# Two token tiles to a numerator matmul, and the order of the loop around it: a hedgehog linear-attention block with a token mixer on one core

## The chip, the core and the metric

The kernel runs on one core of a Trainium2 chip. The metric is the device time of one execution in microseconds (us). Engines: TensorE (PE in the profile, its weight loads PEld), VectorE (DVE), ScalarE (ACT), GpSimd (POOL), and SyncE (SP), which issues most of the transfers. Each engine works through its own list of instructions in order.

## The reference

```
x:    (1, 2048, 512), 32 heads of width 16
q, k, v = layernorm(x) @ wqkv
phi(u)  = [softmax(u @ w_phi), softmax(-(u @ w_phi))]        per head, 32 features
kv, z   = phi(k)^T v, sum of phi(k) over the tokens
num     = phi(q) kv
den     = phi(q) z + 1e-6
h       = x + (num / den) @ wo
u       = gelu(layernorm(layernorm(h))^T @ w1 + b1)          w1: (2048, 1792), along the tokens
out     = h + (u @ w2 + b2)^T                                w2: (1792, 2048)
```

All in float32.

## The kernel before

A token tile is 128 tokens, so there are NT = 16. Most float32 products are made of three matmuls in a faster 32-bit format (`mm3`, L60): each operand is split into a rounded part (`hi`, written by ScalarE) and the remainder (`lo`, a subtraction), and hi·hi, hi·lo and lo·hi are summed.

The first stage (to about 143 us of the span) makes phi(k), kv and z over all tiles, and projects q for some tiles on the way. The last one (from 387 us) is the second mixer product. Between them lies the loop of L630, `for it in range(NT + 3)`, which the change rewrites. It takes every tile through a pipeline, with a different tile at each step of one iteration:

- `q_mm` projects q for a tile (12 matmuls of 512 columns into one of two PSUM buffers, `pu`). Ten of the 16 tiles are left to this stage, six of them to the loop.
- `q_logits` (through `logit_ops`, L137) reads that buffer four times: VectorE takes the maximum (`mx`) and the minimum (`mn`) of each head and writes `v - mx` (the shift); ScalarE copies `v` raw into the other half of the tile (L147), and `negate` on GpSimd turns the copy into `mn - v`. `q_exp` then runs exp over both on ScalarE, and `q_sums` sums them on VectorE.
- `s_ez` (GpSimd) and `s_den` (VectorE: `tz`, `den`, `w`) make the weight that normalizes phi(q) and divides by den at once, and `s_pq` (GpSimd) multiplies phi(q) by it.
- `s_tr` transposes the tile's phi(q) on TensorE (8 transposes into the PSUM tile `tn`, L525), and two ScalarE copies bring it to SBUF as `pht` (L527).
- `s_num` multiplies with kv: 16 matmuls of 64 rows by 32 columns of weights and 128 moving columns, eight of them side by side in the array (L543, again into `tn`). Its result is split into `oh` (ScalarE) and `ol` (VectorE, `s_ol`).
- `s_wo` is the output projection, 12 matmuls of 512 columns into the one buffer `po`. `s_h` adds x and stores h, `s_moments`, `s_rstd` and `s_hn` normalize it and split it into `hs`.
- `fill` is the first mixer product: 12 matmuls for a token tile and a pair `p` of 128-feature blocks. In the loop it fills TensorE's time for pairs 0 and 1, LAG iterations behind the tile; all the rest follows after the loop. `stream` loads two tiles' weights (SP), `whi` is a ScalarE copy (L604), and `flush` makes `wlo` on VectorE (L596). Four buffers each hold `wraw`, `whi` and `wlo`.

From L419 on, `tc.manual_schedule` is in force: TensorE, VectorE, ScalarE and GpSimd execute in the order in which the code records the operations, until the loop ends (`ms.close()`). A framework places the semaphore waits from what each operation reads and writes; where two engines read the same PSUM tile, the one recorded later waits for the one recorded earlier. `turns` interleaves lists of VectorE operations, and `run` records them.

In one iteration TensorE's order is: num(it - 1), wo(it - 2), tr(it), then q_mm or fills.

Of the kernel before, what the change touches and what calls it, by code (L numbers as in the profile page):

```python
# [9 lines left out]
F32 = mybir.dt.float32  # L10
F32R = mybir.dt.float32r
AF = mybir.ActivationFunctionType
# [5 lines left out]
P = 128  # L18
# [4 lines left out]
NG = 8  # L23
# [1 line left out]
Q_AT = (4, 6, 8, 9, 11, 13)  # L25
V_NOT = (0, 1, 11)
SUMS = 8
LAG = 4
WARM = 9
EPS = 1e-5  # L30

# [2 lines left out]
def block_kernel(ctx: ExitStack, tc: tile.TileContext, x, xT, wT, phic, wo, w1, b1, w2, b2,  # L34
# [25 lines left out]
    def mm3(o, ah, al, bh, bl, first, last):  # L60

        nc.tensor.matmul(o, ah, bh, start=first, stop=False)  # L62
        nc.tensor.matmul(o, ah, bl, start=False, stop=False)  # L63
        nc.tensor.matmul(o, al, bh, start=False, stop=last)  # L64
# [72 lines left out]
    def logit_ops(src, e, pool):  # L137

        v = src.rearrange("p (j h d) -> p j h d", h=2, d=DH)
        ev = signs(e)  # L140
        mx = wk.tile([P, NPR, 2], F32, name="mx")
        mn = wk.tile([P, NPR, 2], F32, name="mn")

        def shift():
            nc.vector.tensor_sub(ev[:, :, 0], v, mx.unsqueeze(3).to_broadcast([P, NPR, 2, DH]))
            if pool:
                nc.scalar.activation(ev[:, :, 1], v, AF.Copy)  # L147
                MN.append((ev, mn))
            else:
                nc.vector.tensor_sub(ev[:, :, 1], mn.unsqueeze(3).to_broadcast([P, NPR, 2, DH]), v)  # L150

        return [lambda: nc.vector.tensor_reduce(mx, v, axis=AX.X, op=ALU.max),
                lambda: nc.vector.tensor_reduce(mn, v, axis=AX.X, op=ALU.min),
                shift]
# [7 lines left out]
    def turns(*lists):  # L162

        return [ops[i] for i in range(max(map(len, lists))) for ops in lists if i < len(ops)]

    def run(*lists):
        for op in turns(*lists):
            op()
# [192 lines left out]
    def q_mm():  # L361
        if q["mm"] < NT:
            PS[q["mm"]] = proj(q["mm"], wqh, wql, ps_q, "pu")
            q["mm"] += 1

    def q_logits(lag):
        n = q["logits"]
        if n < min(NT, q["mm"] - lag + NT * (q["mm"] == NT)):
            EQ[n] = big.tile([P, NG, P], F32, name="eq", tag="big")
            q["logits"] += 1  # L370
            return logit_ops(PS[n], EQ[n], n >= len(Q_AT))
        return []
# [71 lines left out]
    def s_den(t):  # L444


        tz = az.tile([P, NPR, 2, 2], F32, name="tz")
        den = az.tile([P, NPR, 2], F32, name="den")
        W[t] = az.tile([P, NPR, 2, 2], F32, name="w", bufs=3)
        other = SQ[t]  # L450
        return [lambda: nc.vector.reduce_sum(tz.rearrange("p g c h -> p (g c h)"), heads(EZ[t]), axis=AX.X),
                lambda: nc.vector.scalar_tensor_tensor(tz[:, :, 0], other[:, :, 1], 1e-6, tz[:, :, 0],
                                                       op0=ALU.mult, op1=ALU.add),
                lambda: nc.vector.tensor_mul(tz, other, tz),
                lambda: nc.vector.reduce_sum(den, tz.rearrange("p g c h -> p g h c"), axis=AX.X),
                lambda: nc.vector.reciprocal(den, den),
                lambda: nc.vector.tensor_mul(W[t], other, den.unsqueeze(2).to_broadcast([P, NPR, 2, 2]))]  # L457

    def s_pq(t):
        nc.gpsimd.tensor_mul(heads(EQ[t]), heads(EQ[t]), W[t].rearrange("p g c h -> p (g c h)").unsqueeze(2).to_broadcast([P, 2 * H, DH]))  # L460

    def lead(it, mm):

        if 0 <= it + 3 < NT:
            s_ez(it + 3)
        negate()
        for _ in range(mm):
            q_mm()
        q_exp(0)
# [49 lines left out]
    HN, HT, PHT, OS, PO, VE = {}, {}, {}, {}, {}, {}  # L519

    def s_tr(t):
        PHT[t] = ak.tile([P, NG, P], F32, name="pht")
        ptr = ps_t.tile([P, 2, 4, P], F32, name="tn")
        for g in range(NG):
            nc.tensor.transpose(ptr[:, g // 4, g % 4, :], EQ[t][:, g, :], ident)  # L525
        for half in range(2):
            nc.scalar.activation(PHT[t][:, half * 4:half * 4 + 4, :], ptr[:, half], AF.Copy)  # L527

    def s_kv():

        pt = ps_o.tile([P, 2, P], F32, name="po")
        for b in range(2):
            nc.tensor.transpose(pt[:, b, :], kvS[:, 2 * b:2 * b + 2, :].rearrange("p n f -> p (n f)"), ident)
        nc.scalar.activation(kvB, pt, AF.Copy)

    def s_num(t):

        pn = ps_t.tile([P, 2, 4, P], F32, name="tn")[:, :, 0:2]
        for b in range(2):
            for c in range(4):  # L540
                for r in range(2):
                    rows, cols = slice(64 * r, 64 * r + 64), slice(32 * c, 32 * c + 32)
                    nc.tensor.matmul(pn[cols, r, b, :], kvB[rows, b, cols], PHT[t][rows, 4 * b + c, :],  # L543
                                     start=True, stop=True, skip_group_check=True)
        oh = ak.tile([P, 2, 2, P], F32R, name="oh")
        ol = ak.tile([P, 2, 2, P], F32R, name="ol")
        nc.scalar.activation(oh, pn, AF.Copy)
        OS[t] = oh, ol, pn

    def s_ol(t):  # L550
        oh, ol, pn = OS[t]
        return [lambda: nc.vector.tensor_sub(ol, pn, oh)]

    def s_wo(t):
        oh, ol, _ = OS.pop(t)
        PO[t] = po = ps_o.tile([P, D], F32, name="po")
        for j in range(4):
            mm3(po, oh[:, j // 2, j % 2, :], ol[:, j // 2, j % 2, :], woh[:, j, :], wol[:, j, :], j == 0, j == 3)

    def s_x(t):  # L560
        HT[t] = ak.tile([P, D], F32, name="h", bufs=4)
        nc.sync.dma_start(HT[t], x[t * P:(t + 1) * P, :])
# [8 lines left out]
    def s_moments(t):  # L571

        junk = ak.tile([P, D], F32, name="hj", bufs=1)
        nc.scalar.activation(VE[t][:, 1:2], VE[t][:, 2:3], AF.Copy, scale=-1.0 / D)
        nc.scalar.activation(junk, HT[t], AF.Square, bias=VE[t][:, 1:2], accum_out=VE[t][:, 3:4])
        nc.scalar.activation(VE[t][:, 0:1], VE[t][:, 3:4], AF.Identity, scale=(1.0 + EPS) / D, bias=eps2)

    def s_rstd(t):
        nc.gpsimd.tensor_tensor(r2[:, t:t + 1], VE[t][:, 0:1], mhalf[:, :1], op=ALU.pow)
        nc.gpsimd.tensor_mul(VE[t][:, 1:2], VE[t][:, 1:2], r2[:, t:t + 1])  # L580
# [12 lines left out]
    def flush():  # L593
        while LATER:
            wl_, raw, wh_ = LATER.pop(0)
            LO.append(nc.vector.tensor_sub(wl_, raw, wh_).ins)  # L596
# [14 lines left out]
    def fill_load(p):  # L611
        if FL[p] < NT:
            WI[p, FL[p]] = stream(w1v, FL[p], 2, p * 256, 256)
            FL[p] += 2

    def fill(p, pool=None):

        t = FN[p]
        FN[p] = t + 1
        if FL[p] <= t:  # L620
            fill_load(p)
            flush()
        if t == 0:
            PU[p] = [pool.tile([P, D], F32, name="pu", tag="pu") for _ in range(2)]
        a, b = WI[p, t - t % 2]
        for c in range(2):
            mm3(PU[p][c], a[:, t % 2, c * P:(c + 1) * P], b[:, t % 2, c * P:(c + 1) * P],
                HN[t][:, 0], HN[t][:, 1], t == 0, t == NT - 1)

    for it in range(NT + 3):  # L630
        if 0 <= it < NT:
            s_x(it)
        if 0 <= it - 1 < NT:
            s_num(it - 1)
        if 0 <= it - 3 < NT:
            s_moments(it - 3)
        if 0 <= it - 2 < NT:
            s_wo(it - 2)
        if it == 1:
            run(q_logits(0))  # L640
            q_mm()
        if 0 <= it < NT:
            s_tr(it)
        if it == 0:
            s_kv()
        if 0 <= it + 1 < NT:
            s_pq(it + 1)
        if 0 <= it - 3 < NT:
            s_rstd(it - 3)
        lead(it, 1)  # L650
        den = s_den(it + 2) if it + 2 < NT else []
        ops = turns((s_ol(it - 1) if 0 <= it - 1 < NT else []) + q_logits(1) + (q_sums(0) if it > 0 else []), den)

        ops[3:3] = ([lambda: s_h(it - 2)] if 0 <= it - 2 < NT else []) + [flush]
        run(ops)
        if it > 0:
            negate()
        if 0 <= it - 3 < NT:
            s_hn(it - 3)
        if FN[0] <= it - LAG:  # L660
            fill(0, ps_f)
        for _ in range(2):
            if q["logits"] == NT and FN[1] <= it - LAG:
                fill(1, ps_q)
        for p in range(2):
            if it >= LAG - 2 and FL[p] <= FN[p] + 1:
                fill_load(p)
    flush()
    ms.close()
# [197 lines left out]
```

## Time and profile before

| what | us |
| --- | --- |
| median of 3 runs (lowest, highest) | 535.25 (534.66, 535.86) |
| the profiled execution | 535.27, its span 533.5 |
| PE, PEld busy | 523.4, 451.0 |
| DVE, ACT, POOL busy | 382.5, 277.6, 228.3 |
| numerators, L543, in the loop | 256 matmuls in 512 records, 0.60 a tile |
| fills, L62 to L64 into `pu` | 672 matmuls, about 0.39 each, started 0.228 apart |
| granted TensorE clock | 0.999 |

The span runs from the first to the last instruction. A matmul's duration holds the time in which it is pipelined with its neighbours, so two starts tell more of the pace than two durations. Line numbers in profile lines are those of the kernel before; in the changed kernel the same statements stand a line or a few lines further down.

### The profile page before, as it was taken

How to read it: one execution, taken by the hardware profiler on the slowest of the kernel's cores; microseconds unless marked ns; L12 is line 12 of the kernel's file. 1: busy time of each engine (PE TensorE's matmuls, PEld its weight loads, DVE VectorE, ACT ScalarE, POOL GpSimd, SP SyncE). 2: the span in 40 equal slices, each digit the busy share in tenths (PEclk: the TensorE clock that was granted, in tenths of full speed). 3: DMA queues.
4: the chain of work that ended last, by engine and by line, in shares of the span. 5: the costliest groups of instructions: out<-in, count | busy, mean ns of one | idle time of the engine just before them, and what ended most of it. 6: DMA issues, size and time to landing. Idle time of an engine off the chain costs nothing.

```text
span 533.5 us, 9887 instructions
## 1 busy us (share of the span) xinstructions
PE 523.4 (98%) x3872; PEld 451.0 (85%) x3872; DVE 382.5 (72%) x680; ACT 277.6 (52%) x470; POOL 228.3 (43%) x180
## 2 busy tenths in 40 slices
PE   8999999999999899999999999999999999999995
PEld 7888888887877777778788888888899999999995
DVE  6893999878798979784235523835768878887784
ACT  6998833525447777666766423525443343343340
POOL 2589699877876978985345000000001101100110
PEclk9999999999999999999999999999999999999999
DMA  8544310022302223333355333533014556535631
GB/s 303 196 124 119 86 35 21 1 62 78 101 1 83 95 81 119 120 109 111 95 159 182 99 100 99 159 111 87 20 41 110 138 149 146 131 120 120 158 78 43
DMA packets 45487, 55.85 MB, mean 105 GB/s; under 512 B 3968, under 2 KB 33024, under 8 KB 45440
## 3 DMA queue, kind: packets, MB, share of 16 engines
q1 hardware_dynamic: 43136, 51.38, 30.3%
q0 software_dynamic: 2016, 3.67, 5.1%
q8 instruction: 30, 0.49, 0.4%
q10 hardware_dynamic: 288, 0.17, 0.1%
q14 instruction: 17, 0.14, 0.1%
HBM read 46.81 MB, written 8.39 MB: 103 GB/s over the span
## 4 chain that ended last, share of the span: by engine, by line
PE 90%; DVE 5%; ACT 3%; issue 1%; POOL 1%; DVEq 0%; ACTq 0%; POOLq 0%
PE py L761 26%; PE pu L62 12%; PE pu L64 12%; PE pu L63 11%; PE po L62 3%; PE pv L63 2%; PE tn L525 2%; PE pv L64 2%; PE pv L62 2%; PE pk_ps L62 2%; PE po L63 2%; PE po L64 2%; PE pk_ps L64 2%; PE pk_ps L63 2%; PE tn L543 2%; PE kvp L207 1%
## 5 line engine op out<-in xcount | busy, mean ns | idle before, releaser
L799 POOL DMA_DIRECT2D out<-ot x14 | 12.5, 1001 | 212.1 <-DVE ot L797 212.1
L761 PE MATMUL py<-uf,whi 128*128 128x256 f32 x560 | 96.2, 283 | 0.0
L62 PE MATMUL pu<-hs,whi 128*128 128x512 f32 x224 | 87.6, 394 | 0.7 <-ACT eq L147 0.7
L57 ACT ACTIVATE whi<-wraw 128x1792 fp32r<-128x1792 f32 x28 | 47.7, 1705 | 77.9 <-PE py L761 62.9
L63 PE MATMUL pu<-hs,whi 128*128 128x512 f32 x224 | 87.2, 389 | 0.0
L64 PE MATMUL pu<-hs,wlo 128*128 128x512 f32 x224 | 87.0, 390 | 0.2 <-DVE wlo L596 0.2
L761 PEld LDWEIGHTS py<-uf,whi 128*128 128x128 f32 x560 | 83.3, 192 | 0.0
L596 DVE TENSOR_TENSOR wlo<-wraw,whi 128x512 fp32r<-128x512 f32 x56 | 46.3, 841 | 45.2 <-ACT whi L604 44.0
L761 PE MATMUL py<-uf,wlo 128*128 128x256 f32 x280 | 69.9, 283 | 0.0
L58 DVE TENSOR_TENSOR wlo<-wraw,whi 128x1792 fp32r<-128x1792 f32 x28 | 56.6, 2023 | 17.8 <-ACT whi L57 17.8
L604 ACT ACTIVATE whi<-wraw 128x512 fp32r<-128x512 f32 x56 | 34.4, 627 | 45.6 <-PE pu L63 41.6
L62 PEld LDWEIGHTS pu<-hs,whi 128*128 128x128 f32 x224 | 42.1, 188 | 9.3 <-ACT eq L147 1.2
L64 PEld LDWEIGHTS pu<-hs,wlo 128*128 128x128 f32 x224 | 42.1, 188 | 9.3 <-DVE wlo L596 0.6
L761 PEld LDWEIGHTS py<-uf,wlo 128*128 128x128 f32 x280 | 49.7, 192 | 0.0
L63 PEld LDWEIGHTS pu<-hs,whi 128*128 128x128 f32 x224 | 42.1, 188 | 8.4
L442 POOL TENSOR_TENSOR ez<-eq,zB 128x1024 f32<-128x1024 f32 x16 | 39.5, 2474 | 0.1
L761 PE MATMUL py<-un,whi 128*128 128x256 f32 x224 | 38.4, 283 | 0.0
L195 POOL TENSOR_TENSOR pk<-pk,sk 128x1024 f32<-128x1024 f32 x16 | 31.1, 1944 | 9.8 <-DVE sk L194 9.0
L460 POOL TENSOR_TENSOR eq<-eq,w 128x1024 f32<-128x1024 f32 x16 | 31.0, 1940 | 5.9 <-DVE w L457 5.9
L527 ACT ACTIVATE pht<-tn 128x512 f32<-128x512 f32 x32 | 17.4, 596 | 30.8 <-PE tn L525 30.8
L761 PEld LDWEIGHTS py<-un,whi 128*128 128x128 f32 x224 | 33.2, 192 | 0.1
L199 POOL TENSOR_TENSOR zacc<-zacc,pk 128x1024 f32<-128x1024 f32 x13 | 31.3, 2406 | 0.6
(165 smaller groups left out, 1192.8 us busy)
## 6 DMA issues: line engine op xcount, KB each, us to landing
wraw<-in_w SPq DMA_DIRECT2D x112, 256.0 KB, 2.9
xraw<-in_xT SPq DMA_DIRECT2D x16, 256.0 KB, 3.1
xh<-in_x SPq DMA_DIRECT2D x16, 256.0 KB, 2.6
h<-in_x SPq DMA_DIRECT2D x16, 256.0 KB, 3.1
out<-h SPq DMA_DIRECT2D x16, 256.0 KB, 2.0
out<-ot POOLq DMA_DIRECT2D x14, 256.0 KB, 4.6
wraw<-in_wT SPq DMA_DIRECT2D x12, 256.0 KB, 5.0
wo<-in_wo SPq DMA_DIRECT2D x4, 256.0 KB, 4.7
```

What stands on the lines that cost most here:

```text
L57: nc.scalar.activation(hi, src, AF.Copy)
L58: lo_engine.tensor_sub(lo, src, hi)
L62: nc.tensor.matmul(o, ah, bh, start=first, stop=False)
L63: nc.tensor.matmul(o, ah, bl, start=False, stop=False)
L64: nc.tensor.matmul(o, al, bh, start=False, stop=last)
L195: nc.gpsimd.tensor_mul(heads(PK[t]), heads(PK[t]), sk.unsqueeze(2).to_broadcast([P, 2 * H, DH]))
L199: nc.gpsimd.tensor_add(zacc, zacc, PK[t])
L442: nc.gpsimd.tensor_mul(EZ[t], EQ[t], zB)
L460: nc.gpsimd.tensor_mul(heads(EQ[t]), heads(EQ[t]), W[t].rearrange("p g c h -> p (g c h)").unsqueeze(2).to_broadcast([P, 2 * H, DH]))
L596: LO.append(nc.vector.tensor_sub(wl_, raw, wh_).ins)
L604: nc.scalar.activation(wh_, raw, AF.Copy)
L761: nc.tensor.matmul(o, a[x], b[:, y], start=start and i == 0, stop=stop and i == 2, skip_group_check=True)
```

## The change

The numerator is made for two token tiles at once: `pht` holds the transposes of a pair, and each of the 16 matmuls moves 256 columns, in every second iteration. The result is evicted by tile (`oh[:, i]`, `ol[:, i]`). `pht`, `oh` and `ol` have one buffer each in place of two.

The loop body is written anew. TensorE's order in an even iteration is num of the last two tiles, q_mm or fills, wo(it - 2), tr(it); in an odd one q_mm or fills, tr(it), wo(it - 2). So a q tile or fills stand between num and wo. The GpSimd product `s_pq` comes first in an iteration. On VectorE the two `ol` halves with the first step of den between them come first after num, then logits, flush and sums interleaved with the rest of den, and `s_h` last. The normalization `s_hn` of two tiles goes to the even iteration, one behind num and one at the end. The raw copy of q is recorded ahead of VectorE's reductions. LAG is 5 in place of 4, weights of pair 1 are asked for two iterations later than those of pair 0 and both one step further ahead, and `fill` flushes whenever the part that it needs is still in LATER.

```diff
-LAG = 4
+LAG = 5
...
     def logit_ops(src, e, pool):
...
+        if pool:
+            nc.scalar.activation(ev[:, :, 1], v, AF.Copy)
 
         def shift():
             nc.vector.tensor_sub(ev[:, :, 0], v, mx.unsqueeze(3).to_broadcast([P, NPR, 2, DH]))
             if pool:
-                nc.scalar.activation(ev[:, :, 1], v, AF.Copy)
                 MN.append((ev, mn))
...
     def s_tr(t):
-        PHT[t] = ak.tile([P, NG, P], F32, name="pht")
+        j, i = divmod(t, 2)
+        if i == 0:
+            PHT[j] = ak.tile([P, NG, 2, P], F32, name="pht", bufs=1)
...
-            nc.scalar.activation(PHT[t][:, half * 4:half * 4 + 4, :], ptr[:, half], AF.Copy)
+            nc.scalar.activation(PHT[j][:, half * 4:half * 4 + 4, i, :], ptr[:, half], AF.Copy)
...
-    def s_num(t):
-        pn = ps_t.tile([P, 2, 4, P], F32, name="tn")[:, :, 0:2]
+    def s_num(j):
+        pn = ps_t.tile([P, 2, 4, P], F32, name="tn")
...
-                    nc.tensor.matmul(pn[cols, r, b, :], kvB[rows, b, cols], PHT[t][rows, 4 * b + c, :],
+                    nc.tensor.matmul(pn[cols, r, 2 * b:2 * b + 2, :], kvB[rows, b, cols], PHT[j][rows, 4 * b + c, :, :],
                                      start=True, stop=True, skip_group_check=True)
-        oh = ak.tile([P, 2, 2, P], F32R, name="oh")
-        ol = ak.tile([P, 2, 2, P], F32R, name="ol")
-        nc.scalar.activation(oh, pn, AF.Copy)
+        oh = ak.tile([P, 2, 2, 2, P], F32R, name="oh", bufs=1)
+        ol = ak.tile([P, 2, 2, 2, P], F32R, name="ol", bufs=1)
+        pv = pn.rearrange("p r (b i) s -> p i r b s", i=2)
+        for i in range(2):
+            nc.scalar.activation(oh[:, i], pv[:, i], AF.Copy)
...
-        return [lambda: nc.vector.tensor_sub(ol, pn, oh)]
+        return [lambda i=i: nc.vector.tensor_sub(ol[:, i], pv[:, i], oh[:, i]) for i in range(2)]
...
     def fill(p, pool=None):
...
         if FL[p] <= t:
             fill_load(p)
+        if any(part is WI[p, t - t % 2][1] for part, _, _ in LATER):
             flush()
...
+    def fills(it):
         if FN[0] <= it - LAG:
             fill(0, ps_f)
         for _ in range(2):
             if q["logits"] == NT and FN[1] <= it - LAG:
                 fill(1, ps_q)
+
+    for it in range(NT + 3):
+        even = it % 2 == 0
+        if 0 <= it + 1 < NT:
+            s_pq(it + 1)
+        if it == 0:
+            s_tr(0)
+            s_kv()
+        if it == 1:
+            run(q_logits(0))
+            q_mm()
+            s_tr(1)
+        if it > 1 and even:
+            if it <= NT:
+                s_num(it // 2 - 1)
+            if it >= 4:
+                s_hn(it - 4)
+        den = s_den(it + 2) if it + 2 < NT else []
+        if it > 1 and even and it <= NT:
+            ol = s_ol(it // 2 - 1)
+            run(ol[:1] + den[:1] + ol[1:])
+            den = den[1:]
+        if it < NT:
+            s_x(it)
+        if it + 3 < NT:
+            s_ez(it + 3)
+        negate()
+        q_mm()
+        fills(it)
+        q_exp(0)
+        logits = q_logits(1)
+        if it >= 3 and even:
+            s_moments(it - 3)
+        if it > 1 and even and it - 2 < NT:
+            s_wo(it - 2)
+        if 1 < it < NT:
+            s_tr(it)
+        if it > 1 and not even and it - 2 < NT:
+            s_wo(it - 2)
+        if it >= 3 and not even:
+            s_moments(it - 3)
+        if it >= 3:
+            s_rstd(it - 3)
+        run(logits + [flush] + (q_sums(0) if it > 0 else []), den)
+        if 0 <= it - 2 < NT:
+            s_h(it - 2)
+        if it > 0:
+            negate()
+        if it >= 3 and even:
+            s_hn(it - 3)
         for p in range(2):
-            if it >= LAG - 2 and FL[p] <= FN[p] + 1:
+            if it >= LAG - 2 + 2 * p and FL[p] <= FN[p] + 2:
                 fill_load(p)
```

The body that it replaces is shown above with the kernel. The number of projections, transposes, output projections and fills is the same in both.

More of the change, by code (lines that the diff above doesn't have):

```diff
@@ L542, in s_num, with s_ol @@
                     rows, cols = slice(64 * r, 64 * r + 64), slice(32 * c, 32 * c + 32)
-                    nc.tensor.matmul(pn[cols, r, b, :], kvB[rows, b, cols], PHT[t][rows, 4 * b + c, :],
+                    nc.tensor.matmul(pn[cols, r, 2 * b:2 * b + 2, :], kvB[rows, b, cols], PHT[j][rows, 4 * b + c, :, :],
                                      start=True, stop=True, skip_group_check=True)
-        oh = ak.tile([P, 2, 2, P], F32R, name="oh")
-        ol = ak.tile([P, 2, 2, P], F32R, name="ol")
-        nc.scalar.activation(oh, pn, AF.Copy)
-        OS[t] = oh, ol, pn
-    def s_ol(t):
-        oh, ol, pn = OS[t]
-        return [lambda: nc.vector.tensor_sub(ol, pn, oh)]
+        oh = ak.tile([P, 2, 2, 2, P], F32R, name="oh", bufs=1)
[3 more added lines that the diff above has]
+            nc.scalar.activation(oh[:, i], pv[:, i], AF.Copy)
+        OS[j] = oh, ol, pv
+    def s_ol(j):
+        oh, ol, pv = OS[j]
+        return [lambda i=i: nc.vector.tensor_sub(ol[:, i], pv[:, i], oh[:, i]) for i in range(2)]
     def s_wo(t):
-        oh, ol, _ = OS.pop(t)
+        oh, ol, _ = OS[t // 2]
+        i = t % 2
         PO[t] = po = ps_o.tile([P, D], F32, name="po")
         for j in range(4):
-            mm3(po, oh[:, j // 2, j % 2, :], ol[:, j // 2, j % 2, :], woh[:, j, :], wol[:, j, :], j == 0, j == 3)
+            mm3(po, oh[:, i, j // 2, j % 2, :], ol[:, i, j // 2, j % 2, :], woh[:, j, :], wol[:, j, :], j == 0, j == 3)
     def s_x(t):
@@ L628, in fill @@
                 HN[t][:, 0], HN[t][:, 1], t == 0, t == NT - 1)
[L630 to L659, printed above, removed]
+    def fills(it):
         if FN[0] <= it - LAG:
```

## The prediction

> **What bounds the kernel now.** I read the page, then the chain, then the timelines of single engines around the loop that the change rewrites (143.7 to 270 us).
>
> ```profile
> span 533.5 us, 9887 instructions
> ...
> PE 523.4 (98%) x3872; PEld 451.0 (85%) x3872; DVE 382.5 (72%) x680; ACT 277.6 (52%) x470; POOL 228.3 (43%) x180
> ...
> PE 90%; DVE 5%; ACT 3%; issue 1%; POOL 1%; DVEq 0%; ACTq 0%; POOLq 0%
> ```
>
> The chain that ended last is TensorE for 90%. Busy time alone does not prove it, so I took the starts of its matmuls in one late iteration (start, duration):
>
> ```profile
> 217.72 0.39 PE L64 MATMUL pu<-hs,wlo 128*128 128x512 f32 x1
> 218.04 0.67 PE L543 MATMUL tn<-pht,kvB 64*32 64x128 f32 x32
> 218.63 0.50 PE L62 MATMUL po<-woh,oh 128*128 128x512 f32 x1
> 218.97 0.40 PE L63 MATMUL po<-wol,oh 128*128 128x512 f32 x1
> 219.21 0.39 PE L64 MATMUL po<-woh,ol 128*128 128x512 f32 x1
> ...
> 221.49 1.03 PE L525 MATMUL tn<-ident,eq 128*128 128x128 f32 x8
> 222.28 0.48 PE L62 MATMUL pu<-hs,whi 128*128 128x512 f32 x1
> ```
>
> A 512-column matmul starts 0.228 after the last one, and the numerators start at 218.04 and 225.19: 7.15 us an iteration without a hole. From 143.7 to the end of the loop I find three holes: before the matmuls at 174.16, 186.55 and 195.31, together 2.76 us over the normal spacing. So any new stall of TensorE in the loop is paid in full. The first iterations are another matter, for there ScalarE, VectorE and GpSimd are nearly full as well:
>
> ```profile
> 144.83 1.09 ACT L527 ACTIVATE pht<-tn 128x512 f32<-128x512 f32 x2 [3.54 <-PE tn L525]
> 145.80 0.39 ACT L534 ACTIVATE kvB<-po 128x256 f32<-128x256 f32 x1
> 146.07 1.16 ACT L171 ACTIVATE eq<-eq,r 128x1024 f32<-128x1024 f32 x1
> 147.31 0.60 ACT L147 ACTIVATE eq<-pu 128x512 f32<-128x512 f32 x1
> ```
> ```profile
> 144.18 0.68 DVE L152 TENSOR_REDUCE mx<-pu 128x32 f32<-128x512 f32 x1
> ...
> 146.60 0.68 DVE L145 TENSOR_TENSOR eq<-pu,mx 128x512 f32<-128x512 f32 x1
> ...
> 148.09 0.23 DVE L457 TENSOR_TENSOR w<-smq,den 128x64 f32<-128x64 f32 x1
> ```
>
> VectorE starts the logits of q tile 9 at 144.18, and ScalarE's raw copy follows the shift. The projection of q tile n+2 reuses the PSUM buffer of tile n, so it waits for whichever of the two reads last.
>
> **The numerator.** One tile now costs 0.60 (218.04 to 218.63). The matmuls before and after it are 0.09 and 0.12 further apart than 0.228, so 0.80 in all, 1.60 for two tiles. The 32 records of L543 come in four waves 0.109 apart for 128 columns; four 512-column float32 records of L487 are 0.429 apart, so the wave is proportional to its columns. At 256 columns four waves add 0.43: 1.03, with the transitions 1.23. Saved 0.37 a pair, 3.0 us over eight pairs. The bounds are free columns (6.4 us saved) and no gain from pairing but the transitions (1.6); L543 with L487 are the nearest rows, so 3.0.
>
> **The eviction behind the numerator** is now two halves on ScalarE (0.55 each) and two on VectorE (0.60) with a 1.13 us reduction between. wo needs the first half only: 0.17 + 0.55 + 0.60 = about 1.4 us after the numerator, covered by twelve matmuls (2.74). Cost 0 while VectorE is on time; without the cover 1.4 a pair. The halves and their reads bring no new bytes. h last: the next wo waits for it through the one po buffer, but 12 fills and a transpose (3.6 us) stand between, cost 0 late in the loop. The loads of x, moved behind the numerator on SP's queue, land in 3.1 us (page) and are wanted more than an iteration later: 0. LAG 5 moves one iteration's 12 fills behind the loop, the same work later: 0. At the end, normalizing the last tile took from 270.10 to 276.68; 42 matmuls (9.6 us) that need other tiles stand behind wo: 0.
>
> **The raw copy ahead of the shift.** In the built program the order turns round: VectorE's first reduction (mx) waits for ScalarE's raw copy, and shift and reduction then hold the PSUM buffer. Behind the waiting mx VectorE's whole list is queued: den, the weights w that GpSimd waits for, the ol halves, h. I laid the queues out by hand from 143.70, with the rows' durations.
>
> S1, iteration 1. ScalarE's copy for tile 9 ends about 147.75 (two pht copies, kvB, exp, copy from the fence). mx starts there instead of 144.18. The shift ends 3.1 us after mx (146.60 + 0.68 - 144.18): 150.9. TensorE ends q tile 10 at 147.72 and now wants q tile 11 at once. Stall 3.2.
>
> S2, iteration 2. w leaves VectorE 4.1 us after mx: 151.9. GpSimd then runs pq (1.9), ez (2.4), negate (1.05): 157.4. ScalarE follows with exp (1.05) and the raw copy of tile 11 (0.6): 159.1; mx to shift 3.1: 162.2. TensorE has done q 11 (2.75), tr (0.8), q 12 (2.9) and num (1.1) since 150.95, and stands before q 13 at 158.55. Stall 3.7.
>
> Then q 14 and q 15 find their shifts done (168.55 against 168.65, 174.6 against 176.3). In iteration 5 the first fill waits 0.6 for its wlo and wo 0.55 for h: 1.15.
>
> S3, iteration 6. The fill of weight pair 1 needs wlo behind both ol halves. From the end of tr(4) at 182.75, ScalarE runs pht (1.0), hn, hs, whi, exp, raw copy: 187.5. Then VectorE runs mx, tz, mn, shift, a wlo, two sums and the small ones of den (6.2 together), h (0.65), ol, tz, ol (2.3), wlo: 197.85. TensorE wants it at 192.0 (after fill, tr, wo, num, fill). Stall 5.9. The row of wlo (L596, in the loop) has a mean of 1.14 and a median of 0.69; the long ones stand beside ez on GpSimd, as these do, so I take the mean; with the median it is 5.4.
>
> S4, iteration 7. Pair 1's second weights are loaded at the end of iteration 6 and used one iteration later: from the end of tr(6), 0.2 + pht 1.0 + hn and hs 1.4 + two whi 1.05, then the second wlo 1.8 later, make 5.5; TensorE asks after 1.9 (six matmuls of pair 0 and two of pair 1). Stall 3.5 (2.6 by the median). Later weights are loaded two iterations ahead.
>
> New stalls: 3.2 + 3.7 + 1.15 + 5.9 + 3.5 = 17.45. They replace the 2.76 of before, since the queues that made those are rearranged. Sum 17.45 - 2.76 - 3.0 = 11.7. The profiled execution took 535.27 (span 533.5 and 1.8 around it), the median is 535.25, so 535.3 + 11.7 = **547.0 us**. Its low end takes free numerator columns (3.4 more saved) and the median wlo (1.4 less): 542.2. Its high end takes the smaller saving (1.4 less) and L596's longest, 2.47, once in S3 and once in S4 (2.7 more): 551.
>
> One rule speaks against the change. The row first: the clock stayed 1.00 over the 1.76 us hole at 172.4, and in the last two stretches of the windows below (columns: PE, PEld, DVE, ACT, POOL, clock, DMA) it falls only in the second, though the last matmul starts near 525.
>
> ```profile
> 525.00:530.00 5.00, 3.09 (x26) 2.88 (x25) 3.96 (x10) 0.38 (x1) 0.00 (x0) 1.00 0.00 0
> 530.00:533.50 3.50, 0.00 (x0) 0.00 (x0) 0.00 (x0) 0.00 (x0) 0.00 (x0) 0.85 0.42 152
> ```
>
> The Trainium skill, "TensorE: Matmul & The Clock Gate", Part 1, says that an idle window of about 3.4 us halves TensorE's clock. By it the holes S2 and S3 could each lose the clock; the trace shows a fall only after more than 5 us of idleness, and nothing of a hole between 1.8 and 5.
>
> **Rivals.**
> - Faster: the raw copy is done before VectorE wants it, and TensorE runs through. 535.3 - 2.8 - 3.0 = 529.5. For it: the copy no longer waits for the shift (ScalarE idled 2.17 before the copy at 170.85). Against it: the copy stands behind exp, which waits for GpSimd's negate, in an in-order queue. It decides if S1 to S4 are together under 5.8 us. Chance 0.06.
> - Half of it: S1 and S2 come, but VectorE catches up before the fills, and S3 and S4 vanish. 535.3 + 6.9 + 1.15 - 5.8 = 537.6. For it: VectorE's list there is den 2.4, logits 1.8, sums 1.3, h 0.65, ol 0.6 and a wlo, some 7.4 us, against 7 of TensorE, so it is close. It decides if wlo comes before 192.0. Chance 0.11.
> - The eviction is late in every pair: h of the odd tile and two wlo push ol, which has 2.74 - 1.4 = 1.3 us to spare, 1 us past its cover in the last five pairs: 552. Against: VectorE was 13.4 busy of 20 at 230 to 250 us. Chance 0.10.
> - One lost clock: at the start of the span 18 records of L288 took 4.21, 0.234 each, where L525's of the same size are 0.109 apart, for about the first 5.7 us. Half speed that long costs 2.9 once: 549.9. For it: S3 is longer than any hole of before but the last. Against it: that last one fell only after more than 5 us. It decides if S3 exceeds what the clock bears, somewhere between 1.8 and 7. Chance 0.13.
>
> **How the numbers follow.** The forecast keeps 0.60: 547.0, its own ends 542.2 and 551. The range 537 to 551 takes in the half case and the lost clock and leaves out the fast case and the late eviction, 0.16. What a measurement can tell from no change is 0.2%, 1.1 us. Faster is the first rival, 0.06. Of the half case 0.03 goes to savings that just cancel its stalls; the other 0.91 is slower.
>
> **What would show it.** The profile after should have q-projection matmuls released by the shift near 151 and 162, and a fill released by wlo near 198, with mx waiting for ScalarE's copy; the numerators of two tiles about 1.03 us long; late pairs 13.9 us apart. I am wrong if the loop's first eight iterations hold no hole above 2 us, or if the late pairs have them.

## The result, and the profile after

The changed kernel takes 563.78 us (median; 562.62 to 564.87) against 534.97 of before: ratio 1.0535, interval 1.051 to 1.056. The forecast was 547.0 with a range of 537 to 551. Its direction was right and its size too small, by 17 us. The profiled execution took 562.62 us, 27.35 more than that of before, and the ledger below is made against it.

The page of the changed kernel: the span, the busy times, the granted clock in 40 slices, and the chain that ended last.

```profile
span 560.8 us, 9395 instructions
PE 529.5 (94%) x3616; PEld 452.8 (81%) x3616; DVE 385.2 (69%) x680; ACT 277.1 (49%) x470; POOL 230.4 (41%) x180
PEclk9999999998989977999999999999999999999999
PE 50%; DVE 1%; DVEq 0%; issue 0%; ACT 0%
```

TensorE went from 98% busy to 94%, and its clock row, full throughout before, now has dips in the tenth to sixteenth slice of 14 us. The first is new idle time (31.3 us of the span against 10.1), the second is time in which matmuls ran more slowly. The chain is followed back through only half of the span (its shares add up to 51%), so I read the rest from the starts of TensorE's matmuls and from the waits.

**The first long hole lies ahead of the loop.** Single engines around 125 us (start, duration, engine, line; in brackets the idle time before and its releaser). First VectorE before the change:

```profile
125.05 1.29 DVE L480 TENSOR_TENSOR zacc<-zacc,pk 128x512 f32<-128x512 f32 x2 [0.41 <-POOL pk L195]
```

The same stretch after it, TensorE, VectorE, ScalarE:

```profile
124.81 0.39 PE L64 MATMUL pv<-wvh,xs 128*128 128x512 f32 x1
129.96 3.50 PE L488 MATMUL pk_ps<-zacc,ones 128*128 128x512 f32 x4 [4.76 <-DVE zacc L481]
```
```profile
126.78 0.69 DVE L153 TENSOR_REDUCE mx<-pu 128x32 f32<-128x512 f32 x1 [4.09 <-ACT eq L144]
...
128.58 1.83 DVE L481 TENSOR_TENSOR zacc<-zacc,pk 128x512 f32<-128x512 f32 x2
```
```profile
125.57 0.69 ACT L187 ACTIVATE vs<-pv,r 128x512 f32<-128x512 f32 x1 [2.14 <-PE pv L64]
126.16 0.59 ACT L144 ACTIVATE eq<-pu 128x512 f32<-128x512 f32 x1
```

Read from the bottom: ScalarE makes `vs`, which waits for the v projection of TensorE; behind it in the queue stands the raw copy (126.16); VectorE's maximum waits 4.09 us for that copy; the two additions into `zacc` stand behind the logits on VectorE and so run at 128.58 instead of 125.05; and TensorE, which has nothing else in its queue ahead of the sums of `zacc`, stands from 124.81 to 129.96. The loop's first transposes start at 149.47 instead of 143.70, 5.8 us late.

**In the loop**, the waits of the changed kernel between 149 and 300 us (in total, times, longest):

```profile
DVE mx L153 <- ACT eq L144: 11.5, 5, 5.4
PE pu L64 <- DVE wlo L603: 7.4, 2, 5.3
PE pu L62 <- DVE eq L147: 5.2, 2, 3.1
PE pu L62 <- ACT whi L611: 2.2, 1, 2.2
```

VectorE waits for the raw copy, TensorE for the shift (twice), for low weights (twice) and high weights (once). These are S1, S2, S3 and the two holes of S4 of the prediction. TensorE's matmuls behind them:

```profile
156.69 0.50 PE L62 MATMUL pu<-wqh,xs 128*128 128x512 f32 x1 [3.12 <-DVE eq L147]
...
168.01 0.50 PE L62 MATMUL pu<-wqh,xs 128*128 128x512 f32 x1 [2.09 <-DVE eq L147]
...
202.92 0.79 PE L64 MATMUL pu<-hs,wlo 128*128 128x512 f32 x1 [5.30 <-DVE wlo L603]
...
215.38 0.66 PE L62 MATMUL pu<-hs,whi 128*128 128x512 f32 x1 [2.18 <-ACT whi L611]
...
218.58 0.80 PE L64 MATMUL pu<-hs,wlo 128*128 128x512 f32 x1 [2.11 <-DVE wlo L603]
```

From start to start these holes are 3.51, 2.46, 5.69, 2.58 and 2.74 us.

Three more holes stand ahead of wo in the late pairs, 1.40, 2.14 and 0.83 us from start to start. The first of them on VectorE, then TensorE:

```profile
235.79 3.70 DVE L603 TENSOR_TENSOR wlo<-wraw,whi 128x512 fp32r<-128x512 f32 x2 [1.91 <-ACT whi L611]
...
243.25 0.68 DVE L575 SCALAR_TENSOR_TENSOR h<-po,h 128x512 f32<-128x512 f32 x1
```
```profile
244.09 0.47 PE L62 MATMUL po<-woh,oh 128*128 128x512 f32 x1 [1.01 <-ACT hs L57]
```

The even tile's wo needs the one po buffer, which the odd tile's h frees at 243.94; h stands last on VectorE behind two low weights, the sums and the denominator. The profile puts the wait down to `hs`, which ends at 244.03, the later of two candidates by 0.1 us. But in all three pairs wo starts 0.15 us behind the end of h, while `hs` ends 0.06, 0.04 and 0.83 us ahead of it, so h is the likely cause; the run with another order, number 5 below, settles it.

**The clock.** Stretches of 3.41 us of the changed kernel (columns: length, busy PE, PEld, DVE, ACT, POOL, granted clock, DMA share, GB/s):

```profile
126.82:130.23 3.41, 0.27 (x1) 0.30 (x2) 3.41 (x5) 0.00 (x0) 1.06 (x1) 1.00 0.00 0
154.13:157.54 3.41, 0.85 (x4) 0.72 (x5) 3.31 (x9) 0.07 (x1) 0.00 (x0) 1.00 0.00 0
198.50:201.91 3.41, 0.00 (x0) 0.00 (x0) 3.38 (x7) 3.19 (x7) 3.22 (x3) 1.00 0.64 227
201.91:205.32 3.41, 2.40 (x6) 1.92 (x7) 3.24 (x9) 0.00 (x0) 3.41 (x3) 0.50 0.29 80
212.15:215.56 3.41, 1.23 (x6) 0.70 (x5) 0.72 (x1) 3.38 (x7) 1.19 (x1) 1.00 0.41 153
256.52:259.93 3.41, 1.84 (x9) 1.18 (x7) 3.21 (x11) 1.40 (x3) 2.45 (x4) 1.00 0.29 77
```

Behind the first, second, third and fifth of these the clock stood at 0.50: for 3.41 us from 130.23 and from 157.54, for 6.83 from 201.91 and from 215.56. Behind the last, in which TensorE was busy for 1.84 us, it stayed at 1.00.

**The ledger** (holes less the normal spacing of 0.23):

| part | us |
|---|---|
| loop starts late (hole 4.9 against 0.6 of before, 3.41 us at half clock behind it) | 5.8 |
| S1 3.28, S2 2.23, iteration 5 0.18 (wlo) + 0.57 (h), S3 5.46, S4 2.35 + 2.51 | 16.6 |
| late h in three pairs: 1.17, 1.91, 0.60 | 3.7 |
| half clock in the loop: TensorE busy 3.41 + 5.82 + 4.72 in the three stretches, half of it | 7.0 |
| holes of before that went | -2.8 |
| numerator, 8 pairs at 0.37 | -3.0 |
| sum (measured 27.35) | 27.3 |

### The profile page after: what moved, and what is told of

Its sections match the earlier page's. It is cut to its first block, busy times and chain, and to the rows that moved or that the text cites. A ratio compares the mean times of both kernels' runs of the same rounds, so it can differ in the third digit from the quotient of the medians.

```text
span 560.8 us, 9395 instructions
## 1 busy us (share of the span) xinstructions
PE 529.5 (94%) x3616; PEld 452.8 (81%) x3616; DVE 385.2 (69%) x680; ACT 277.1 (49%) x470; POOL 230.4 (41%) x180
## 4 chain that ended last, share of the span: by engine, by line
PE 50%; DVE 1%; DVEq 0%; issue 0%; ACT 0%
PE py L790 25%; PE pu L62 7%; PE pu L64 7%; PE pu L63 7%; PE po L62 1%; PE po L64 1%; PE po L63 1%; PE tn L528 0%; PE tn L547 0%; DVE hb L841 0%; DVEq L892 0%; DVE hb L842 0%; DVE hb L839 0%; DVE hb L837 0%; ACT e L836 0%
## 5 line engine op out<-in xcount | busy, mean ns | idle before, releaser
L64 PE MATMUL pu<-hs,wlo 128*128 128x512 f32 x224 | 88.6, 398 | 7.4 <-DVE wlo L603 7.4
L603 DVE TENSOR_TENSOR wlo<-wraw,whi 128x512 fp32r<-128x512 f32 x56 | 50.6, 913 | 61.7 <-ACT whi L611 61.2
L62 PE MATMUL pu<-hs,whi 128*128 128x512 f32 x224 | 88.5, 400 | 2.2 <-ACT whi L611 2.2
L63 PE MATMUL pu<-hs,whi 128*128 128x512 f32 x224 | 88.3, 395 | 0.0
L461 POOL TENSOR_TENSOR eq<-eq,w 128x1024 f32<-128x1024 f32 x16 | 32.8, 2052 | 17.6 <-DVE w L458 17.6
L62 PE MATMUL pu<-wqh,xs 128*128 128x512 f32 x64 | 27.8, 435 | 5.2 <-DVE eq L147 5.2
```

## The experiments

All are built on the changed kernel unless a line says otherwise. Single times are compared with 563.8 us, the changed kernel's median; before measured 534.9 to 535.2 us beside them. Numbers 1, 2, 3, 7, 8 and 9 ran once, and the changed kernel's four executions lie 2.25 us apart, so smaller differences between single times are read from the traces alone.

**1. The raw copy back behind the shift.**

```
-        if pool:
-            nc.scalar.activation(ev[:, :, 1], v, AF.Copy)
         def shift():
             ...
             if pool:
+                nc.scalar.activation(ev[:, :, 1], v, AF.Copy)
                 MN.append((ev, mn))
```

> The changed kernel with one edit undone: the raw copy of q is recorded behind the shift again. Theory A (the early copy makes ScalarE's queue a gate for VectorE): the hole of 5.15 us before the matmuls of zacc near 125 us and the two holes before q projections (3.5 and 2.5 us) go, and with them the two half-clock stretches that start at 130 and 157 us; the holes before the fills of pair 1 stay. 562.6 - 5.8 - 5.5 - 1.7 = about 550 us. Rival B (the new loop order makes the holes, whoever copies first): only the hole near 125 us goes, 557 us.

551.83 us, 12.0 less. The hole ahead of the loop is as before again (0.84 from start to start) and S1 and S2 are gone. One q projection further on, in iteration 3 behind the transposes of iteration 2, a new hole of 1.77 opens (number 11 closes it). S3 and S4 stay, at 4.67 and 2.35 + 2.63 us. That is what the theory with the copy as one cause among several had forecast (about 550).

**2. The kernel before, with the copy ahead of the shift and nothing else.** (The same lines, moved the other way.)

> The kernel before with one part of the change alone: the raw copy of q ahead of the shift. Theory A: the hole before the matmuls of zacc appears here too, with a half-clock stretch, 5.8 us, and holes before q projections in the first iterations of the loop; 541 to 550 us. Rival B: the copy alone costs only the hole near 125 us and the loop hides the rest, at most 541 us.

557.72 us, 22.8 over before: more than either theory allowed. Besides the 5.15 us hole ahead of the loop, the order of before pays in nearly every iteration that makes q logits. TensorE in it:

```profile
158.10 0.50 PE L62 MATMUL pu<-wqh,xs 128*128 128x512 f32 x1 [2.52 <-DVE eq L148]
...
170.87 1.06 PE L527 MATMUL tn<-ident,eq 128*128 128x128 f32 x8 [1.90 <-DVE ol L554]
...
190.15 1.30 PE L527 MATMUL tn<-ident,eq 128*128 128x128 f32 x8 [2.10 <-DVE ol L554]
```

VectorE stands at the maximum, so ol and h behind it are late too, and TensorE waits for these. The longest wait in the loop, 4.16 us, stands ahead of the fill at 207.44, whose buffer the last shift frees. In the old order one moved instruction costs 22.8 of the 28.8 us by itself; the new order of the loop softens its effect (undoing it there saves 12.0) and adds losses of its own.

**3. The weights early.**

```
-            if it >= LAG - 2 + 2 * p and FL[p] <= FN[p] + 2:
+            if it >= LAG - 2 and FL[p] <= FN[p] + 2:
```

> The changed kernel with weights of pair 1 asked for from the same iteration on as those of pair 0. If the holes before the fills (5.7, 2.6 and 2.7 us) come from weights that are asked for too late, they go, with the two half-clock stretches of 6.83 us that they started: 562.6 - 10.3 - 5 = about 547 us. If they come from VectorE's backlog behind the early copy, they stay: 560 us or more.

554.54 us, 9.2 less, between the two expectations: S3 and S4 are gone from the trace, with the 13.7 us at half clock behind them (one stretch of 3.41 us comes anew behind a late wo). S1 stays at 3.27; the clock no longer falls behind it but behind S2, which grows to 3.75.

**4. Both edits.**

> Both edits in one: the copy behind the shift, weights of pair 1 early. If the two causes are apart, the gains add: 562.6 - 13 - 15 = about 534.5 us, with three holes of 0.6 to 1.9 us left before wo in late pairs; the pairing itself then saves about 3 us. If the same backlog was counted twice, 538 us or more.

540.74 us (540.26 to 541.25), 1.0109 of before (1.0092 to 1.0125). Together the two save 23.0 us, 1.8 more than their single savings of 12.0 and 9.2, which is within what single times can tell. The time lies where the rival had it, but not for the rival's reason: the savings add up, so no backlog was counted twice; each was smaller than the 13 and 15 us forecast. Copy and weights are most of the loss, but not all of it. No stretch below full clock is left in the loop. TensorE starts the loop as before did (the same matmul at 144.48, before at 144.63) and ends it 5.4 us later. What remains is 1.77 us ahead of the q projection of iteration 3 (the only one in that iteration; some of the expectations below call it the second) and the wait for h: 1.18 and 0.73 us ahead of wo in iterations 5 and 6 and 1.83, 1.96, 1.91 and 0.56 in the late pairs.

**5. Another order on VectorE**, on top of 4.

```
-        run(logits + [flush] + (q_sums(0) if it > 0 else []), den)
-        if 0 <= it - 2 < NT:
-            s_h(it - 2)
+        qs = q_sums(0) if it > 0 else []
+        h = [lambda: s_h(it - 2)] if 0 <= it - 2 < NT else []
+        if it > 6 and not even:
+            run(qs, den)
+            run([lambda: flush(1)] + h + [flush])
+        elif logits and it != 3:
+            run(logits + [flush] + h + qs, den)
+        else:
+            run(logits + [flush] + qs, den)
+            run(h)
```

(`flush(n)` issues the first n low weights.)

> The kernel with the raw copy behind the shift and the weights early, 540.74 us, and on top another order on VectorE: where q logits are made, h directly behind the low weights instead of last; in the odd iterations from 7 on the denominator first, then one pair's low weights, h, the other pair's. Theory (h stands last, po has one buffer, so wo of the next even iteration waits for it): the waits ahead of wo in that kernel's trace, 1.18 and 0.71 us at the fifth and sixth and 1.91, 1.99, 1.95 and 0.59 later, 8.3 us in all, go but for 1 to 1.5 us: 533 to 534 us, that is no slower than before. Rival (VectorE has no room there, the low weights at 1.85 us each are what is late): the waits move to the fill or to ol, 538 us or more.

536.2 us (535.73 to 536.65), 1.0018 of before (1.0009 to 1.0028). The four late waits ahead of wo are gone from the trace, which shows that h caused them: in the first of these pairs h now ends at 201.88, wo starts at 204.57 without a wait, and `hs` ends only at 206.27. The gain is 4.5 us, not 7: TensorE now waits 1.15 us for ol in iteration 6, 1.06 ahead of the numerator before it, and twice 0.8 for the low half of `hs`. So the rival (room on VectorE) is partly right.

**6. The evictions of the transposed q tile behind the q logits on ScalarE**, on top of 5. `s_tr` only lists them, and they are issued behind `run(...)` in the iterations that make logits.

> The same order, and the two evictions of the transposed q tile are issued on ScalarE behind the q logits instead of ahead of them. Theory (the 1.97 us ahead of the second q projection of iteration 3 is the raw copy standing in ScalarE's queue behind an eviction that waits for transposes issued late): 1.5 to 2.0 us below the run of the same call without this edit. Rival (the wait is the shift's own, or the later eviction holds up the numerator by as much): no difference within 0.3 us, or slower.

535.74 us (533.89 to 537.1), 1.0009 of before (0.9997 to 1.0022). The 2.00 us hole went as the theory had it. But the numerator of iteration 6 now waits for the late eviction of iteration 5, 2.96 us, in a window in which the clock then falls for 3.41 us. Loss and gain nearly cancel there. It hangs on the clock: in eight of the 11 executions the mean clock was 0.993 to 0.996 and the time 535.4 to 537.1, in the other three 0.998 or 0.999 and 533.9 to 534.3. Only one execution has a trace, so where the clock fell in the others is not shown.

**7. The copy behind the shift ahead of the loop only.**

```
-        if pool:
+        if pool and q["ahead"]:
             nc.scalar.activation(ev[:, :, 1], v, AF.Copy)
...
+    q["ahead"] = True
     for it in range(NT + 3):
```

(and in `shift` the copy where `q["ahead"]` is false.)

> The changed kernel, with the raw copy back behind its shift in the logits made ahead of the loop and ahead of it in the loop. Theory (the hole of 5.15 us ahead of the zacc sums is VectorE's maximum waiting for the raw copy, which waits on ScalarE; the loop then starts 5.8 us late, and the loop's own holes are other waits): 557 us (556 to 558), loop starting at 143.7. Rival (whoever starts the loop early waits the longer in it for the same shifts): 561 us or more.

557.4 us, 6.4 less, as the theory had it. The loop's own holes barely moved: S1 3.27, S3 5.46, S4 2.36 + 2.38; S2 grew from 2.23 to 3.77 us, and the clock fell behind it instead of behind S1. So the part of the loss that the prediction never looked at is a part of its own, not a stall that the loop would have had anyway.

**8. and 9. Dummy matmuls in the holes**, to keep TensorE busy while it waits:

```
+    def spin(o, n):
+        for _ in range(n):
+            nc.tensor.matmul(o, ident, ident, start=True, stop=True, skip_group_check=True)
```

called with an accumulator that is overwritten later, in four places: ahead of the zacc sums, of q tile 11, of pair 1's first fill, and between the fills of iteration 7.

> The changed kernel with extra matmuls of the identity into accumulators that are overwritten later, placed where TensorE waits: 42 of them (4.5 us) ahead of the zacc sums, 27 (2.9 us) ahead of the second q projection of iteration 1, 46 (4.9 us) ahead of the first fill of pair 1, 40 (4.3 us) between the fills of iteration 7; what TensorE waits for is left as it is. Theory (the granted clock of 0.50 for 3.4 to 6.8 us behind each long hole costs time of its own, 8.2 us in all): the four stretches at half clock go or shrink, and the time falls to 553 to 556 us though TensorE has more to do. Rival (the clock only slows what would wait anyway, the holes are the whole cost): 562 us or more.

571.89 us. This was a failure of my arithmetic: an identity matmul of this kind takes 0.22 us, not 0.107, the dummies overran the holes by as much again, and the run says nothing on the question.

> The same test as with the longer dummies, whose identity matmuls took 0.22 us each (10.70 - 1.4 us over 42) and so overran the holes: now 20, 13, 22 and 19 of them in the four places, 4.4, 2.9, 4.8 and 4.2 us, less than the 4.9, 3.3, 5.5 and 4.8 us that TensorE waits there. Theory (half clock behind a hole costs 8.2 us of its own): no stretch at 0.50 behind these four places, and 553 to 556 us. Rival (the clock costs nothing beyond the holes): 562 us or more.

557.9 us, 4.7 less than the changed kernel's profiled execution, although TensorE had 74 matmuls more to do. The stretch that stood at 0.50 in the changed kernel, at the same times in this run:

```profile
201.91:208.74 6.83, 6.45 (x33) 5.07 (x32) 3.85 (x10) 0.00 (x0) 3.74 (x4) 1.00 0.14 40
```

So the half clock costs time of its own. It is less than the 8.2 us of the theory: the loop starts 1.63 us earlier, but S2 then grows from 2.23 to 3.80 us, the clock falls behind that hole instead (166.75 to 170.17), and the numerator of iteration 4 starts at 180.82 against 180.98. The gain that stays, 4.5 us, comes from S3 and S4. Time won ahead of a fixed wait is lost in it.

**10. and 11. One eviction only.** Number 6 had closed one hole and opened another. With `if it != 3: evict()` behind `s_tr(it)` (and the two sums of iteration 5 moved behind the next ol) only one eviction is issued late.

> The kernel with evictions behind the logits lost 1.97 us of waiting in iteration 3 and gained 2.96 us of waiting plus 1.7 us at half clock in iteration 5, where the numerator then waits for the later eviction. Here the eviction is put behind the logits in iteration 3 alone, and the two sums of iteration 5 behind the next ol, which came 1.15 us late for wo. Theory: 535.74 - 2.96 - 1.7 + 1.06 (the wait ahead of that numerator in the kernel without late evictions) - 0.5 = 531.5 to 533 us, faster than before by 0.4 to 0.6%. Rival (each hole closed opens the next one on VectorE or ScalarE, nothing is left over for the pairing): 535 us or more.

535.65 us (535.15 to 535.98), 1.0013 of before (1.0004 to 1.0022). I had picked the wrong iteration: the hole of 2.00 us from start to start stood there as before, the wait ahead of the numerator of iteration 6 was back at 1.06. The transposes ahead of that hole are those of iteration 2:

> The eviction that goes behind the logits is now that of iteration 2 (the run before moved that of iteration 3, and its trace still had the hole of 2.00 us ahead of the second q projection of iteration 3, behind the transposes of iteration 2). Theory (the raw copy stood in ScalarE's queue behind that eviction): the hole of 2.00 us goes, 535.65 - 1.77 = 533.9 us, 0.2% below before. Rival (the time comes back as a wait for the numerator in iteration 4): 535 us or more.

533.3 us (533.04 to 534.1), 0.9963 of before (0.9949 to 0.9976). ScalarE in number 4 and here:

```profile
162.12 1.08 ACT L528 ACTIVATE pht<-tn 128x512 f32<-128x512 f32 x2 [4.40 <-PE tn L526]
163.09 0.60 ACT L146 ACTIVATE eq<-pu 128x512 f32<-128x512 f32 x1
```
```profile
161.56 0.60 ACT L146 ACTIVATE eq<-pu 128x512 f32<-128x512 f32 x1 [3.46 <-DVE eq L144]
162.50 1.09 ACT L533 ACTIVATE pht<-tn 128x512 f32<-128x512 f32 x2 [0.34 <-PE tn L528]
```

The raw copy had stood behind an eviction that waited 4.40 us for transposes, and now runs when its shift is done. This kernel is faster than both, 0.4% under before: it keeps the two-tile numerator and the new order of the loop, and takes back or mends most of what made TensorE wait (the longest holes left in the loop are 1.06 us ahead of a numerator and two of 0.8 for the low half of `hs`). Its span is 532.3 us with TensorE at 98%.

**12. The high weights behind the numerator's evictions**, on top of 11, from iteration 6 on; the low weights follow behind the denominator of the even iteration.

> On top of that, from iteration 6 on, the high weights are made on ScalarE behind the numerator's two evictions of the next even iteration (not ahead of the transposed q tile's evictions of the odd one), and the low weights on VectorE behind the denominator of that even iteration. Theory (the numerator's 0.95, 0.65 and 0.62 us waits of the steady pairs are q evictions standing behind the high weights): about 1.5 us less than the other kernel of this call, 532 to 533 us. Rival (low weights then contend with GpSimd ahead of h, or the weights come late for the fill): no gain, 534 us or more.

534.42 us (533.32 to 535.76), 0.9986 of before (0.9974 to 0.9998), 1.1 us over number 11. Much of that is the clock: six executions with a mean clock of 0.999 or 1.0 took 533.3 to 534.4 us (median 533.6), five with 0.995 or 0.996 took 535.3 to 535.8. Even the six are no faster than number 11. The waits for q evictions went, but the low weights come too late for the fills: TensorE waits 2.08 and 1.05 us for them. VectorE:

```profile
205.51 2.90 DVE L613 TENSOR_TENSOR wlo<-wraw,whi 128x512 fp32r<-128x512 f32 x2
```

The rival holds: no gain. I had counted on the weights being wanted later than they are.

## Why the prediction was right or wrong

**Right: the numerator.** 1.03 us was forecast for a pair:

```profile
225.11 1.09 PE L547 MATMUL tn<-pht,kvB 64*32 64x256 f32 x32
226.14 0.50 PE L62 MATMUL pu<-hs,whi 128*128 128x512 f32 x1
```

From start to start it is 1.03 (its first record at 225.11, the fill at 226.14), so the cost follows the moving columns and the saving is 0.37 a pair. The one late pair without a wait, 225.11 to 239.04, takes the 13.9 us that were forecast; the three behind it take 15.28, 16.01 and 14.70.

**Right in place, uneven in size: S1 to S4.** Forecast 3.2, 3.7, 1.15, 5.9 and 3.5; measured 3.28, 2.23, 0.75, 5.46 and 4.86. Numbers 1 and 3 show that the causes are the ones named: the copy's place makes S1 and S2, the late loads make S3 and S4. In number 7, whose loop starts on time, the matmuls forecast near 151, 162 and 198 start at 150.38, 161.68 and 198.08.

S2 came out 1.5 short because TensorE, at half clock behind S1, came later to the same wait: in numbers 3, 7 and 9, where the clock did not fall behind S1, S2 measured 3.75 to 3.80. S4 came out 1.4 long because of its low weights: the second was counted 1.8 us behind the high weights and ended 3.2 behind them (215.32 to 218.52), the two taking 3.68 us. These two misses cancel, so that the sum fits, 17.45 against 16.6, is luck in part.

**Wrong: where the laying out began.** The step that failed first is "from 143.7 to the end of the loop I find three holes" and the sentence "I laid the queues out by hand from 143.70". The edit of the raw copy is in a helper that is called ahead of the loop too. There, the same mechanism (mx waits for the copy, and VectorE's list behind it) hits the additions into zacc, for which TensorE has no cover. It cost 5.8 us, and number 7, which takes back that call's copy alone, saves 6.4.

**Wrong: "h last ... cost 0 late in the loop".** The cover was counted from wo to wo on TensorE (3.6 us); what was not counted is VectorE's list ahead of h in an odd iteration: two low weights that take 3.70 us beside GpSimd, then 3.8 us of sums and denominator (239.41 to 243.25). wo starts 0.15 us behind the end of h, and is late by 0.6 to 1.9 us in three pairs, 3.7 in all. The longest, 2.14 us from start to start, all but meets the prediction's own sign of being wrong, late pairs with holes above 2 us. In number 4, with the other stalls gone, five pairs pay. The rival with a late eviction had the right list on VectorE and the right number of late pairs for number 4, but the wrong victim: ol is late too (it ends at 244.54 in the pair shown), yet wo stops at h first.

**Wrong: the clock.** It was held at 1.00 in the sum, with one fall of 2.9 us as a rival at 0.13, because the trace of before was read as showing a fall only after more than 5 us of idleness. That reading was wrong: the last matmul of before starts at 527.81, not near 525, and ends at 528.09 (the row shown has 3.09 us of TensorE in it), and the clock fell at 532.43, so 4.3 us of idleness were enough, which did not rule out a fall behind S3. In the changed kernel it fell four times. By TensorE's busy time in the slow stretches that is 1.7 us ahead of the loop (within the 5.8) and 7.0 in it. Of the two ways to read it, the rule from the Trainium skill, "TensorE: Matmul & The Clock Gate", Part 1 (an idle window of about 3.4 us halves the clock), was the better one: the clock fell behind S1 and S3, holes of 3.5 and 5.7 us from start to start, and behind the 5.2 us ahead of the loop. By the Trainium skill's rule alone S4, two holes of 2.6 and 2.7 us, would have kept it, and did not. The same part of the Trainium skill's page adds that the window runs freely at 3413 ns. This trace agrees: the four slow stretches begin 27.31, 44.37 and 13.65 us apart, which is 8, 13 and 4 times 3.413. Of the four windows ahead of the falls TensorE was idle throughout in only one (198.50); in the others it was busy for 0.27 to 1.23 us, so a hole need not fill a window to cost the clock.

Together the missed parts are 5.8 + 3.7 + 7.0 = 16.5 us, against an error of 27.35 - 11.7 = 15.6; the stalls that were laid out were 0.9 too high together, and no one of them was off by more than 1.5.

**What stays open.** The single parts are not independent (in numbers 3, 7 and 9 the clock kept behind S1 comes back as a longer S2 with a fall behind it), so the ledger splits the loss by place, not by edit. Number 11 gained 2.35 us over number 10 in the medians, where the closed hole was 1.77: the two profiled executions lie 1.87 apart (534.1 and 535.97), so the trace accounts for nearly all of that, and the rest is within the spread of the executions. What decides between keeping and losing the clock after a window that is about half idle is open too.

## What to carry to other kernels

When an edit sits in a helper, list its call sites and lay out the queues at each; the call outside the loop cost 5.8 us here. An instruction put ahead in an in-order queue must be asked for its own releaser: whoever waits for it inherits what stands ahead of it, and passes the wait to all behind. Close holes in the order in which they are met, since a gain ahead of a fixed wait is lost there, and price a hole of TensorE with the half clock behind it.

## What the runs showed of the hardware

The clock changed only on a grid: in each of the fourteen traces all its changes lie whole multiples of 3.413 us apart. In the traces of the changed kernel and of the twelve experiments, between 102 and 300 us, every full-speed window in which TensorE was idle for 2.08 us or more (61% to 100% of it) was followed by half clock, and none with 1.67 us or less was. Between 1.71 and 1.87 us it went both ways: 1.85 us from 164.4 left the clock of the changed kernel alone, 1.75 us in number 1 and 1.71 in number 3 halved it. What tells these apart stays open. Once at half, the clock came back after a window with at most 0.3 us idle, and stayed down after windows with 0.7 us and more, which is why it stood at half for 6.83 us behind S3 and behind S4.

A low weight of 128x512 on VectorE took 0.68 to 0.70 us by itself. In the fourteen traces, between 143 and 280 us, each that started while GpSimd was in the middle of making `ez`, `eq` or `hs` ended about 0.55 us behind the end of that GpSimd instruction: it waited for it rather than running more slowly beside it. GpSimd at 235 to 241 us in the changed kernel:

```profile
236.55 2.39 POOL L461 TENSOR_TENSOR eq<-eq,w 128x1024 f32<-128x1024 f32 x1
```

Of the two low weights from 235.79 the first took 1.35 us and the second, from 237.06, 2.42: it ended at 239.48, 0.54 behind this product. Two of 0.69 would have ended 2.3 us sooner, more than the 1.9 that wo was late at most. So by this estimate GpSimd's work, not VectorE's list alone, pushed h past its cover; no run took it away.
